# Chunked attention with a softplus feed-forward layer: the seven output products in another order, w_out's sums on GpSimd, output quarters on its queue

## The chip, the core and the metric

The kernel runs on one core of one Trainium2 chip. The metric is the device time of one execution in microseconds (us); lower is better. The engines are PE (TensorE, matrix products), DVE (VectorE), ACT (ScalarE), POOL (GpSimd) and SP, which here only issues transfers. A name with a small q behind it (SPq, ACTq, POOLq) is an engine's instruction queue, from which transfers are issued in order.

## The reference

Attention is taken within chunks of 64 positions; its output, as 4608 rows of 512, goes through a feed-forward layer of width 2048 with softplus.

```python
scores = scale * np.matmul(q_c, k_c.transpose(0, 1, 2, 4, 3))
scores = scores - np.max(scores, axis=-1, keepdims=True)
attn = np.exp(scores)
attn = attn / (np.sum(attn, axis=-1, keepdims=True) + 1e-09)
out = np.matmul(attn, v_c)
...
h = x @ w_in
g = np.maximum(h, 0.0) + np.log1p(np.exp(-np.abs(h)))
return (g @ w_out).astype(np.float32)
```

## The kernel before

Every float32 product is made of three: an operand is split into a rounded part (hi, cast by ScalarE) and a remainder (lo, a subtraction on VectorE or GpSimd), and hi·hi + lo·hi + hi·lo are summed in PSUM. The 4608 rows are nine blocks of 512. Three blocks are done plainly (`gemm1`, `gemm2`); the other six in three stages of two blocks each, n = 0, 1, 2. In a stage the first product, x @ w_in, is done by a scheme with seven products of half-size operands instead of eight: `product(w, k)`, task P0 to P6, for eight pairs j = 0 to 7 of w_in's column blocks. Its operands are seven sums of x (`x_sum`, `x_hi`, `x_lo`; tasks xs, xH, xL, kept in `wi_hi`/`wi_lo` for k below 4 and in three of the four `wib` tiles above) and seven sums of w_in that lie in a DRAM scratch and are loaded for each pair from GpSimd's queue (`ring_load`, line 745). `mix` (line 807; two of its six sums on GpSimd, the others on VectorE) puts each pair's products together, `soft` (line 816) applies softplus; in stages 0 and 1 the second block's result is spilled to DRAM, loaded back (`spill_load`, line 825, task ul, on SP's queue), and goes through `gemm2` (task G2, its remainder by line 660) after the eight pairs.

The last stage, n = 2 (`BOTH`), does the second product, g @ w_out, by seven products too: `sum_product(k, j)`, line 947, task R{k}_{j}, k = 0 to 6, eight j each. Its g operands are made in place from the four softplus blocks of pair j, u_block(j, i, c) (`t_sum`, line 904, tasks ts1 to ts4; `g_hi`, line 927; `g_lo`, line 931). Its w_out operands are: the plain halves, and four sums per j (`v_total`, line 871, task vt, two per j; `v_sum`, line 881, vs0 to vs3; `v_hi`, line 885, on ScalarE; `v_lo`, line 890, vl0 to vl3). VectorE makes all vt; vs and vl go to GpSimd for even j, to VectorE for odd j. Sum 0 stays in SBUF (`first_image`) for R1; the other sums (`v_store`, line 893, task vd) and copies of the plain halves (`own_image`, line 866) go to a DRAM tensor, `images`, and are loaded back per product (`image_load`, line 897, task wr) on SP's queue. The tiles `eT`, `qe`, `ka` and `ends` hold the sums, and later softplus blocks of pairs 5 to 7.

PE's order is written out as `seq`. In stage 2 it is, per pair j: P0 to P6, one of the two G2 left over from stage 1 (behind pair 0 and pair 1), and for j above 1 R0 and R1 of j - 2. Behind pair 7: R0, R1 of 5, 6 and 7, then R2 to R5, then R6 in two column halves, whose last piece is cut in two (RZ0, RZ1). Two PSUM accumulators of two tiles are shared (`ACC`); `set_by` (task keep), `combine` (sum) and `out_turn` (turn, line 975, a transpose on VectorE) take the four output quarters from them: b after R3, d after R4, a after R5, c21 after R6. `out_store` (line 986, task put) stores a quarter's half `ct` in four transfers of 64 KB, in runs of 32 floats. All of b, d, a and the first half of c21 go from SP's queue; the last half, in two parts of 32 KB transfers, alternately from SP and ACT.

All other engines' orders come from class `Plan`: it runs through the tasks with given costs and urgencies (`urg`, lower first) and emits each engine's instructions in the order that this gives. The order of emission is fixed in the kernel; an engine waits at the instruction that stands next.

## Time and profile before

| what | us |
|---|---|
| median of 3 runs | 841.07 |
| lowest, highest | 840.05, 845.37 |
| the profiled execution | 840.33 |
| its span, from the first to the last instruction | 838.5 |
| PE busy in it | 808.7 (96%) |
| VectorE, ScalarE, GpSimd busy | 594.8, 404.5, 343.9 |

Times in the profile count from the span's start. Busy PE includes matmul ends that are modelled. A chain of waits is followed back from the last instruction, at each step to what released it; in this profile 81% of it is PE. "Idle before" in a group is the time that the engine stood idle just ahead of it, with what ended it.

### The profile page before, as it was taken

What the parts mean: (1) busy time and instruction counts of PE and PEld (TensorE: products, weight loads), DVE (VectorE), ACT (ScalarE), POOL (GpSimd) and SP (SyncE); (2) the same over time, 40 slices, a digit from 0 to 9 for tenths busy, and PEclk for the clock granted to TensorE, in tenths of its full rate; (3) what the DMA queues carried; (4) which work ended last, traced back from release to release, by engine and by line L of the source; (5) the groups of instructions that cost most, each with busy time, mean ns of one, the idle gap of its engine ahead of it and who ended that gap; (6) DMA issues with size and microseconds to landing.
All of it is one profiled execution on the core that took longest, in us unless ns stands there. A gap on an engine that the chain in (4) does not pass through costs nothing.

```text
span 838.5 us, 15563 instructions
## 1 busy us (share of the span) xinstructions
PE 808.7 (96%) x5675; PEld 660.2 (79%) x5675; DVE 594.8 (71%) x985; ACT 404.5 (48%) x667; POOL 343.9 (41%) x395
## 2 busy tenths in 40 slices
PE   8799999999999999999999999999999999899994
PEld 6687878887878888887888878888888777687883
DVE  4898985267477778565578886574777999748771
ACT  3767855443434574353443543444345454545450
POOL 1567569778975712212324111311303376321000
PEclk9999999999999999999999999999999999999998
DMA  9986758642674455776569647678374387753573
GB/s 214 249 222 172 219 147 272 183 113 72 176 171 114 106 155 203 203 214 169 164 199 226 169 139 223 169 208 215 118 229 138 112 303 286 250 174 115 165 187 51
DMA packets 215677, 151.27 MB, mean 180 GB/s; under 512 B 173296, under 2 KB 190960, under 8 KB 211376
## 3 DMA queue, kind: packets, MB, share of 16 engines
q1 hardware_dynamic: 204048, 101.37, 45.2%
q0 software_dynamic: 10464, 48.77, 17.8%
q8 instruction: 45, 0.74, 0.4%
q14 instruction: 32, 0.26, 0.1%
q10 hardware_dynamic: 1088, 0.13, 0.1%
HBM read 106.95 MB, written 41.94 MB: 178 GB/s over the span
## 4 chain that ended last, share of the span: by engine, by line
PE 81%; DVE 8%; ACT 3%; DMA 2%; SPq 2%; issue 2%; POOL 0%; DVEq 0%; POOLq 0%; ACTq 0%
PE po L1006 32%; PE pa L788 22%; PE pa L644 14%; PE po L947 9%; PE pa L608 2%; SPq L359 2%; PE pa L520 1%; DVE wib L807 1%; DVE g_lo L660 1%; DMA xb<-scratch 1%; DMA raw<-in_moe_w_out_dram 1%; DVE ends L881 1%; DMA spill<-ends 1%; DVE raw L871 0%; DVE g_lo L931 0%
## 5 line engine op out<-in xcount | busy, mean ns | idle before, releaser
L807 POOL TENSOR_TENSOR wib<-wib 128x512 f32<-128x512 f32 x48 | 64.8, 1349 | 232.8 <-ACT wib L794 211.3
L1006 PE MATMUL po<-late,g_hi 128*128 128x512 f32 x420 | 128.8, 392 | 0.0
L544 DVE STREAM_TRANSPOSE eT<-qe 32x256 f32<-32x256 f32 x216 | 93.9, 435 | 3.0
L788 PE MATMUL pa<-wi_hi,xb 128*128 128x512 f32 x304 | 94.1, 391 | 1.8 <-DVE wib L807 0.7
L1006 PEld LDWEIGHTS po<-late,g_hi 128*128 128x128 f32 x420 | 78.3, 188 | 16.4
L788 PE MATMUL pa<-wib,xb 128*128 128x512 f32 x360 | 87.2, 395 | 1.9 <-ACT wib L794 1.2
L1006 PE MATMUL po<-late,g_lo 128*128 128x512 f32 x224 | 83.7, 391 | 2.6 <-DVE g_lo L660 2.6
L1006 PE MATMUL po<-wo_hi,g_hi 128*128 128x512 f32 x224 | 85.0, 396 | 0.0
L1006 PE MATMUL po<-wo_lo,g_hi 128*128 128x512 f32 x224 | 83.7, 390 | 0.0
L1006 PE MATMUL po<-wo_hi,g_lo 128*128 128x512 f32 x224 | 83.7, 390 | 0.0
L788 PEld LDWEIGHTS pa<-wib,xb 128*128 128x128 f32 x360 | 66.0, 188 | 20.2 <-ACT wib L794 6.2
L652 ACT ACTIVATE u<-pa 128x512 f32<-128x512 f32 (+1 forms) x50 | 29.0, 581 | 99.9 <-PE pa L644 93.0
L807 DVE TENSOR_TENSOR wib<-wib,pa 128x512 f32<-128x512 f32 x72 | 49.4, 686 | 33.9 <-PE pa L788 19.6
L656 ACT CAST g_hi<-ends 128x512 fp32r<-128x512 f32 x64 | 39.5, 616 | 65.4 <-PE po L1006 57.4
L660 DVE TENSOR_TENSOR g_lo<-ends,g_hi 128x512 fp32r<-128x512 f32 x64 | 45.7, 714 | 33.4 <-ACT g_hi L656 33.2
L788 PEld LDWEIGHTS pa<-wi_hi,xb 128*128 128x128 f32 x304 | 56.8, 188 | 14.9 <-DVE wib L807 1.2
L794 ACT COPY wib<-pa 128x512 f32<-128x512 f32 x72 | 39.8, 587 | 50.9 <-PE pa L788 50.9
L788 PE MATMUL pa<-wi_lo,xb 128*128 128x512 f32 x152 | 59.2, 389 | 0.0
L660 DVE TENSOR_TENSOR g_lo<-u,g_hi 128x512 fp32r<-128x512 f32 (+1 forms) x32 | 32.5, 1015 | 29.3 <-ACT g_hi L656 23.7
L1006 PEld LDWEIGHTS po<-late,g_lo 128*128 128x128 f32 x224 | 42.1, 188 | 12.4 <-DVE g_lo L660 3.7
L1006 PEld LDWEIGHTS po<-wo_hi,g_lo 128*128 128x128 f32 x224 | 42.1, 188 | 8.8
L1006 PEld LDWEIGHTS po<-wo_lo,g_hi 128*128 128x128 f32 x224 | 42.2, 188 | 8.6
(332 smaller groups left out, 1736.1 us busy)
## 6 DMA issues: line engine op xcount, KB each, us to landing
xb<-scratch POOLq DMA_DIRECT2D x19, 1024.0 KB, 5.9
xb<-scratch POOLq DMA_DIRECT2D x20, 768.0 KB, 7.1
raw<-in_moe_w_in_dram SPq DMA_DIRECT2D x16, 512.0 KB, 5.2
raw<-in_moe_w_out_dram SPq DMA_DIRECT2D x16, 512.0 KB, 4.5
scratch<-ends SPq DMA_DIRECT2D x16, 512.0 KB, 3.1
out_dram<-raw SPq DMA_DIRECT2D x28, 256.0 KB, 4.1
spill<-ends SPq DMA_DIRECT2D x14, 512.0 KB, 4.8
ends<-spill SPq DMA_DIRECT2D x14, 512.0 KB, 4.5
```

The costliest lines, as they stand in the source:

```text
L359: eng.dma_start(dst[p0 : p0 + rows], src[b, :, s0 : s0 + rows, :].rearrange("h s d -> s h d"))
L544: nc.vector.transpose(live["eT", i][d : d + BL, tb], e[s : s + BL, kb])
L608: nc.tensor.matmul(pa[o, a, col : col + C], vt[r, 4 * j + 2 * h2 + c2, :], eT[r, :, 4 * c2 + 2 * j + h2, :], start=True, stop=True,)
L644: nc.tensor.matmul(ph, wt[:, c, :], x[:, ts_, c, :], start=(n == 0), stop=(n == 3 * KC - 1))
L652: nc.scalar.activation(w["u"], w["ph"], AF.Softplus)
L656: nc.scalar.copy(w["hi"], w["u"])
L660: (nc.gpsimd if pool else nc.vector).tensor_tensor(w["lo"], w["u"], w["hi"].bitcast(F32), op=ALU.subtract)
L788: nc.tensor.matmul(w["bank"][BANK[k]], wts[:, q, c, :], x[:, c, :], start=k < NX and c + n == 0, stop=c == 1 and n == 2, skip_group_check= ...
L794: nc.scalar.copy(tmp_of(n), w["bank"][n])
L807: (nc.gpsimd if what in MIX_POOL else nc.vector).tensor_tensor(out, a, b, op=op)
L947: nc.tensor.matmul(live["acc", ACC[k]][ct][:, cols], (w[:, q] if k > 1 else w[q])[:, ct * P : (ct + 1) * P], g[:, cols], start=k in (0, 1, ...
L1006: nc.tensor.matmul(pos[w["m"]][t], terms[n][0][:, j * P : (j + 1) * P], terms[n][1], start=(w["first"] and n == 0), stop=n == 2 and (w["la ...
```

## The change

- `sum_product` takes as k = 0 and k = 1 the two plain halves of w_out, `wo[2j]` and `wo[2j + 1]`, with u_block(j, 0, 0) and u_block(j, 1, 0) as they come out of softplus. The products with sums are k = 2 to 5, and k = 6 has the plain half once more from `images`. ts1 to ts4 now serve k = 2, 3, 5 and 6. The accumulators are shared in another order (`ACC`, `set_by`, `combine`).
- R1 and R0 of pair j - 1 stand behind pair j (before: of j - 2), both left-over G2 behind pair 0, and R1, R0 of 6 and 7 behind pair 7. R5 of the last three j is split by output half (`SPREAD`).
- All vt, vs and vl go to GpSimd. For j = 0 to 3 they are made once P5 and P6 of stage 1's last pair are done, in `wib1` and `wib2`, the tiles that then take the sums of x of k = 5 and 6 for stage 2; these wait for the stores vd of j = 0 to 3. For j = 4 to 7 they are made in the three `raw` tiles, once the output rows of the last block of stage 1 are stored. All four sums of a j are stored now, and vs of a j waits for the stores of the j before it in its stage. `own_image` stores only half of what it did.
- The softplus blocks lie elsewhere: pair 0 in `ends`, pair 1 in `eT` and `qe`, pair j above 1 in w_out's tiles of j - 2.
- Quarters a, c, d (c in place of b) are stored from GpSimd's queue, c21 alternately from SP's and ACT's.

The diff, cut to its core:

```diff
+    SUM_OF = (2, 3, 5, 4)
+    def own_image(j, q):
+        on("wo").dma_start(images[6, :, j, q, :], wo[2 * j + 1][q].bitcast(F32)[:, HC:])
...
+    def v_space(j):
+        at = SUM_AT[j]
+        if ("v space", at) not in live:
+            if at in SUM_RAW:
+                live["v space", at] = [raw_tile(n, True) for n in range(3)]
+                a, b = (later.tile([P, 4 * MT], F32, name=f"wib{n}") for n in (1, 2))
+                live["v space", at] = [a[:, : 2 * MT], a[:, 2 * MT :], b[:, : 2 * MT], b[:, 2 * MT :]]
+        return live["v space", at]
...
-        live["vt", j, b] = raw_tile(0)[:, b * DM : (b + 1) * DM] if j % 2 else blk_tile("eT")
-        nc.vector.tensor_tensor(live["vt", j, b], hi, lo, op=ALU.add)
+        space = v_space(j)
+        t = space[j % (len(space) - 2)]
+        live["vt", j, b] = t[:, b * DM : (b + 1) * DM]
+        (nc.vector if j in VT_DVE else nc.gpsimd).tensor_tensor(live["vt", j, b], hi, lo, op=ALU.add)
...
-        t = ends.bitcast(F32)[:, n * MT : (n + 1) * MT] if j % 2 else blk_tile(("qe", "ka")[n % 2])
+        t = v_space(j)[n // 2 - 2][:, n % 2 * MT : (n % 2 + 1) * MT]
-        (nc.vector if j % 2 else nc.gpsimd).tensor_tensor(live["vs", j, n][:, 1], a, b, op=op)
+        (nc.vector if j in V_DVE else nc.gpsimd).tensor_tensor(live["vs", j, n][:, 1], a, b, op=op)
...
-    OF_G = ((0, 0), (0, 0), (0, 0), (1, 1), (0, 1), (1, 0), (0, 0))
+    OF_G = ((0, 0), (1, 0), (0, 0), (0, 0), (1, 1), (0, 1), (1, 0))
-    ACC = (0, 1, 0, 1, 0, 1, 0)
+    ACC = (0, 1, 1, 0, 1, 0, 0)
...
-            w = (wo[2 * j], [first_image(j)[:, q] for q in range(2)])[k]
+            w = wo[2 * j + k]
...
-                start=k in (0, 1, 5) and j == 0 and n < len(cts), stop=j == FC // 2 - 1 and n >= 2 * len(cts),
+                start=k < 3 and j == 0 and n < len(cts), stop=j == FC // 2 - 1 and n >= 2 * len(cts),
...
-        nc.scalar.copy(saved(what, ct), live["acc", 1 if what == "d" else 0][ct])
+        (nc.vector.tensor_copy if what == "a" and ct else nc.scalar.copy)(
+            saved(what, ct), live["acc", int(what != "c")][ct]
+        )
...
-        nc.vector.tensor_tensor(to, to, saved("c", ct) if what == "d" else live["acc", 1][ct], op=ALU.add)
+        nc.vector.tensor_tensor(to, to, live["acc", int(what == "c")][ct], op=ALU.add)
...
+    def put_queue(what, ct, cb):
+        return PUT[what, ct][cb % len(PUT[what, ct])]
...
-        eng = nc.sync if part is None else (nc.sync, nc.scalar, nc.sync, nc.scalar)[cb]
+        eng = {"ACT": nc.scalar, "SP": nc.sync, "POOL": nc.gpsimd}[put_queue(what, ct, cb)]
...
+    SUM_AT = (1, 1, 1, 1, 2, 2, 2, 2)
+    SUM_RAW = (2,)
+    VT_DVE = ()
+    V_DVE = ()
+    R_LAG = 1
+    SPREAD = 3
+    VD_URG = 60
+    OWN_URG = -100
+    PUT = {(w, ct): ("POOL",) for w in "acd" for ct in range(2)}
+    PUT.update({("c21", ct): ("SP", "ACT") for ct in range(2)})
...
-            seq += [f"G2_{v_['name']}" for v_ in behind[1:]] if n not in BOTH else []
-            if n in BOTH and w["j"] > 1:
-                seq += [f"R{k}_{w['j'] - 2}" for k in range(2)]
-            behind = behind[1:] if n in BOTH else w["first"][::-1]
+            seq += [f"G2_{v_['name']}" for v_ in behind[1:]]
+            if n in BOTH and R_LAG <= w["j"] < FC // 2 - 1:
+                seq += [f"R{k}_{w['j'] - R_LAG}" for k in (1, 0)]
+            behind = [] if n in BOTH else w["first"][::-1]
...
-            seq += [f"R{k}_{FC // 2 - 2 + j}" for j in range(2) for k in range(2)]
-            seq += [f"R{k}_{j}" for k in range(2, 6) for j in range(FC // 2)]
+            NJ = FC // 2
+            seq += [f"R{k}_{j}" for j in range(NJ - R_LAG - 1, NJ) for k in (1, 0)]
+            seq += [f"R{k}_{j}" for k in range(2, 6) for j in range(NJ if k < 5 else NJ - SPREAD)]
+            seq += [f"R5_{j}{ct}" for ct in range(2) for j in range(NJ - SPREAD, NJ)]
...
+            if k > 4:
+                gone = gone + [f"vd{j}_{i}" for j in range(FC // 2) if SUM_AT[j] == n - 1 and n - 1 not in SUM_RAW for i in range(4)]
...
+                if j > 1:
+                    needs += [f"R{i}_{j - 2}", f"vt{j - 2}_{i}"] + [f"own{j - 2}{q}" for q in range(2)] * i
+                elif j:
+                    needs += [f"B{tag(list(bursts)[-1])}_{b}" for b in range(2)]
                 else:
-                    needs += [f"v{'d' if f else 'l'}{FC // 2 - 1 - b}_{f}" for b in range(2) for f in range(4)]
+                    needs += [f"lo{v_['name']}" for w_ in pairs[at - FC // 2 : at] for v_ in w_["second"]]
...
+            d = due((at, 1, 0)) + 8 * nth if at not in SUM_RAW else A + 25 + 10 * nth
+            eng, cost = ("DVE", 0.42) if j in V_DVE else ("POOL", 0.75)
+            if at in SUM_RAW:
+                free = [f"st{SUPERS[n] - 1}_{t}" for t in range(TPM)] + [f"B{tag(list(bursts)[-1])}_{i}" for i in range(2)]
+                free += [f"x{q}{n}_0" for q in "HL"]
+                wide = 1
+            else:
+                free = [f"P{k}_{pairs[FC // 2 * (at + 1) - 1]['name']}" for k in (5, 6)]
+                wide = 2
             for b in range(2):
-                plan.add(f"vt{j}_{b}", "DVE", 0.69, partial(v_total, j, b), [f"w_{h}{of_out[2 * j + b]}" for h in ("hi", "lo")] + before_, urg=d)
+                needs = [f"w_{h}{of_out[2 * j + b]}" for h in ("hi", "lo")] + free
+                if nth >= wide:
+                    needs += [f"vs{mine[nth - wide]}_{i}" for i in range(4)]
+                pool = j not in VT_DVE
+                plan.add(f"vt{j}_{b}", "POOL" if pool else "DVE", 1.4 if pool else 0.69, partial(v_total, j, b), needs, urg=d)
...
+                needs += [f"vd{mine[nth - 1]}_{i}"] if nth else []
...
-                if i:
-                    plan.add(f"vd{j}_{i}", QUEUE["wo"], ISSUE[QUEUE["wo"]], partial(v_store, j, i), [f"vl{j}_{i}"], urg=d + 5, kb=215)
+                plan.add(f"vd{j}_{i}", QUEUE["wo"], ISSUE[QUEUE["wo"]], partial(v_store, j, i), [f"vl{j}_{i}"], urg=d + VD_URG, kb=215)
...
-                t = {1: 1, 2: 2, 4: 3, 6: 4}.get(k)
+                t = {2: 1, 3: 2, 5: 3, 6: 4}.get(k)
...
-                        past = {2: ["keepa0", "keepa1"], 3: ["keepd0", "keepd1"], 4: ["keepb0", "keepb1"], 5: ["sumb0", "sumb1"],
-                                6: ["keepc0", "keepc1"]}
+                        past = {2: ["keepa0", "keepa1"], 3: ["suma0", "suma1"], 4: ["keepd0", "keepd1"], 5: ["keepc0", "keepc1"], 6: [f"sumd{ct}"]}
...
+            for what, end, urg in (("a", f"R0_{e}", B + 2), ("c", f"R4_{e}", B + 36), ("d", f"R5_{e}{ct}", -3)):
+                plan.add(f"sum{what}{ct}", "DVE", 0.69, partial(combine, what, ct), [end, f"keep{what}{ct}"], urg=urg)
+                plan.add(f"turn{what}{ct}", "DVE", 0.66, partial(out_turn, what, ct),
+                         [f"sum{what}{ct}"] + [f"vd{j}_{i}" for j in range(NJ) if SUM_AT[j] in SUM_RAW for i in range(4)], urg=urg + 4 if urg > 0 else B + 50)
                 for cb in range(4):
-                    plan.add(f"put{what}{ct}{cb}", "SP", 0.57, partial(out_store, what, ct, cb), [f"turn{what}{ct}"], urg=1e5, kb=100)
...
-            plan.add(f"putc210{cb}", "SP", 0.57, partial(out_store, "c21", 0, cb), ["turnc210"], urg=1e5, kb=100)
-                eng = ("SP", "ACT", "SP", "ACT")[cb]
+                    eng = put_queue(what, ct, cb)
+                    plan.add(f"put{what}{ct}{cb}", eng, ISSUE[eng], partial(out_store, what, ct, cb), [f"turn{what}{ct}"], urg=1e5, kb=100)
```

## Rows read from the trace of the kernel before

**Rows 1.** Stretches: length, busy PE, PEld, DVE, ACT, POOL (count), clock, DMA, GB/s

```profile
641.00:661.93 20.93, 19.99 (x109) 16.07 (x100) 20.91 (x19) 11.82 (x19) 11.58 (x8) 1.00 0.50 161
661.93:763.65 101.72, 97.75 (x422) 77.95 (x421) 79.38 (x113) 50.18 (x100) 50.37 (x54) 1.00 0.63 222
763.65:827.04 63.39, 63.38 (x279) 51.60 (x278) 45.23 (x71) 30.55 (x54) 0.00 (x0) 1.00 0.48 137
```

**Rows 2.** Timeline after 815, three engines: start, us, engine, line, operation, out<-in

```profile
817.13 1.30 DVE L975 STREAM_TRANSPOSE raw<-wib 128x512 f32<-128x512 f32 x2
...
817.87 13.79 SPq L986 DMA_DIRECT2D out_dram<-raw  x8
...
827.55 1.89 ACTq L986 DMA_DIRECT2D out_dram<-k  x4
...
833.94 1.94 SPq L986 DMA_DIRECT2D out_dram<-k  x4
```

**Rows 3.** Waits of SP's queue after 600: total us, times, longest us

```profile
SPq L825 <- DVE g_lo L660: 26.8, 6, 7.0
...
SPq L986 <- DMA out_dram<-k: 9.9, 1, 9.9
```

**Rows 4.** Waits of PE, 640 to 728, columns as before

```profile
PE pa L788 <- ACT wib L794: 1.9, 2, 1.2
...
PE pa L788 <- DVE wib L807: 1.1, 2, 0.7
...
PE pa L788 <- ACT ends L885: 1.0, 1, 1.0
```

**Rows 5.** Busy time of lines 871, 881, 890 alone, 661.93 to 722.50

```profile
661.93:722.50 60.57, 14.84 (x14) 1.00 0.71 259
...
661.93:722.50 60.57, 9.22 (x16) 10.13 (x12) 1.00 0.71 259
...
661.93:722.50 60.57, 7.14 (x16) 10.13 (x12) 1.00 0.71 259
```

**Rows 6.** Chain of waits, 750 to 764: start us, us, what

```profile
751.24 2.76 PE po L947 x12
...
754.00 9.65 PE pa L788 x42
```

**Rows 7.** Timeline of VectorE, 750 to 756

```profile
754.66 0.69 DVE L931 TENSOR_TENSOR g_lo<-eT,g_hi 128x512 fp32r<-128x512 f32 x1 [1.21 <-ACT g_hi L927]
```

**Rows 8.** GpSimd's groups, 120 to 340: busy us, mean ns; idle before

```profile
L716 POOL TENSOR_TENSOR ends<-raw 128x256 f32<-128x256 f32 x32 | 24.8, 805 | 0.6
...
L704 POOL TENSOR_TENSOR raw<-wi_hi,wi_lo 128x512 f32<-128x512 f32 x8 | 10.2, 1286 | 0.9 <-DMA scratch<-raw 0.8
```

**Rows 9.** Busy time, 120 to 300, columns as in Rows 1

```profile
120.00:300.00 180.00, 176.18 (x1556) 145.14 (x1546) 115.91 (x201) 81.77 (x127) 142.55 (x173) 1.00 0.58 154
```

**Rows 10.** Line 660, whole run: duration ns min/median/max

```profile
L660 DVE TENSOR_TENSOR g_lo<-ends,g_hi x64: 653/692/1227, 328.3 to 662.4; 128x512 fp32r<-128x512 f32 x64
...
L660 DVE TENSOR_TENSOR g_lo<-u,g_hi x32: 414/693/4783, 32.1 to 315.0; 128x512 fp32r<-128x512 f32 x29, 128x256 fp32r<-128x256 f32 x3
```

**Rows 11.** Line 881 on GpSimd, whole run: duration ns min/median/max

```profile
L881 POOL TENSOR_TENSOR qe<-eT x8: 742/876/1646, 642.7 to 712.1; 128x256 f32<-128x256 f32 x8
...
L881 POOL TENSOR_TENSOR ka<-eT,ka x4: 720/939/1710, 648.8 to 713.5; 128x256 f32<-128x256 f32 x4
```

**Rows 12.** Start of the third stage: timeline of VectorE

```profile
665.95 1.22 DVE L775 TENSOR_TENSOR wib<-xa,wib 128x1024 fp32r<-128x1024 f32 x1
```

**Rows 13.** Line 893's stores, whole run: time from issue to landing

```profile
DMA to landing us min/median/max: 2.0/4.3/7.1
```

**Rows 14.** GpSimd's DMA issues of lines 371 and 479: ns min/median/max

```profile
L371 POOL DMA_DIRECT2D raw<-in_v_dram x28: 617/618/656, 146.4 to 442.9; - x28
...
L479 POOL DMA_DIRECT2D k<-in_k_dram x1: 1127/1127/1127, 102.6 to 102.6; - x1
```

**Rows 15.** Line 745's loads, GpSimd's queue: time from issue to landing

```profile
DMA to landing us min/median/max: 4.6/6.3/10.0
```

More of the change, by code (lines that the diff above doesn't have):

```diff
@@ L219, in chunked_attention_softplus_ffn @@
     wi = [tuple(const.tile([P, HALF_FC, KC, P], F32R, name=n) for n in ("wi_hi", "wi_lo"))]
-    stage = [later.tile([P, 4 * MT], F32, name="wib") for _ in range(4)]
+    stage = [later.tile([P, 4 * MT], F32, name=f"wib{n}") for n in range(4)]
     wo = [tuple(const.tile([P, DM], F32R, name=f"wo_{n}{fc}") for n in ("hi", "lo")) for fc in range(HALF_FC)]
@@ L313, in wi_of @@
         if n == len(wi):
-            wi.append(tuple(later.tile([P, 4, KC, P], F32R, name="wib") for _ in range(2)))
+            wi.append(tuple(later.tile([P, 4, KC, P], F32R, name=f"wib{2 * n - 2 + i}") for i in range(2)))
         return [w[:, fc - (0, HALF_FC, HALF_FC + 4)[n]] for w in wi[n]]
@@ L670, in high @@
     def high(n):
-        if "high" not in live:
-            live["high"] = [later.tile([P, 4 * MT], F32R if j < 3 else F32, name="wib") for j in (0, 1, 2, 3)]
-        return live["high"][n]
+        if ("high", n) not in live:
+            live["high", n] = later.tile([P, 4 * MT], F32R if n < 3 else F32, name=f"wib{n}")
+        return live["high", n]
     def x_image(k):
@@ L1470, in add_sums @@
         NJ = FC // 2
-        gone = [f"B{tag(list(bursts)[-1])}_{i}" for i in range(2)]
         for j in range(NJ):
             for q in range(2):
-                for b in range(1, 2):
-                    plan.add(f"own{j}{q}{b}", QUEUE["wo"], ISSUE[QUEUE["wo"]], partial(own_image, j, q, b),
-                             [f"w_{'lo' if q else 'hi'}{of_out[2 * j + b]}", f"G2_{pairs[FC // 2 * (j // 4)]['second'][0]['name'] + 4 * (j % 4) + 2 * q}"], urg=A - 200 + 3 * j, kb=225)
+                plan.add(f"own{j}{q}", QUEUE["wo"], ISSUE[QUEUE["wo"]], partial(own_image, j, q),
+                         [f"w_{'lo' if q else 'hi'}{of_out[2 * j + 1]}", f"G2_{pairs[FC // 2 * (j // 4)]['second'][0]['name'] + 4 * (j % 4) + 2 * q}"], urg=A + OWN_URG + 3 * j, kb=115)
@@ L1507, in add_sums @@
                 else:
-                    needs = [f"own{j}{q}{int(k > 0)}" for q in range(2) for j in half]
-                end = f"R{k}_{half[-1]}" if k < 6 else ("R6_31", "RZ1")[part]
+                    needs = [f"own{j}{q}" for q in range(2) for j in half]
+                end = f"R{k}_{half[-1]}" + ("1" if (k, part) == (5, 1) else "") if k < 6 else ("R6_31", "RZ1")[part]
                 plan.add(f"wr{k}_{part}", QUEUE["image"], ISSUE[QUEUE["image"]], partial(image_load, k, part), needs + ([f"wr{k}_0"] if part else []),
@@ L1564, in add_sums @@
[L1564 to L1571 removed]
+            for what, k in (("a", 1), ("d", 2), ("c", 3)):
+                on_dve = what == "a" and ct
+                plan.add(f"keep{what}{ct}", "DVE" if on_dve else "ACT", 0.69 if on_dve else 0.6, partial(set_by, what, ct),
+                         [f"R{k}_{e}"] + ([f"P4_{last}", f"c11_{last}", f"soft00_{last}", f"soft11_{last}"] if k == 1 else []), urg=-4)
@@ new lines, in add_sums @@
+        for ct in range(2):
+            for z in range(2) if ct else (None,):
+                name = "c21" + str(ct) + ("" if z is None else "ab"[z])
+                plan.add("turn" + name, "DVE", 0.75 if z is None else 0.45, partial(out_turn, "c21", ct, z), [f"R6_{e}0" if z is None else f"RZ{z}"], urg=-3)
+                for cb in range(4):
+                    eng = put_queue("c21", ct, cb)
+                    plan.add(f"put{name}{cb}", eng, ISSUE[eng], partial(out_store, "c21", ct, cb, z), ["turn" + name], urg=1e5, kb=50 if ct else 100)
```

115 lines of the change are left out of this document (35 added, 80 removed).

## Prediction

> **What bounds the kernel now.** Read the page first: PE is busy almost throughout, so time can come only from the gaps of PE and from what lies behind its last product. The table by stretch shows where these are [rows 1]. From 763.65 PE runs 63.38 of 63.39 us: R2 to R6 have no gap and give nothing. From 661.93 to 763.65, the eight pairs of the last stage, PE is busy 97.75 of 101.72. From 641 to 661.93, the last G2 of stage 1, it loses 0.94. And after PE's last product, at 827.04, 11.46 us pass to the end of the span, 838.5.
>
> Next, the timeline of the end [rows 2]. SP's queue holds eight stores of quarter a from 817.87 for 13.79 us; then come the first half of c21 and, last, four stores of its second half, until 833.94 + 1.94 = 835.88. ACT's queue, which had nothing ahead, issued its own four by 827.55 + 1.89 = 829.44. The waits of SP's queue say why [rows 3]: one store on SP waited 9.9 us for a store of c21 on ACT to land, a transfer of a later quarter. So SP stood until c21's end was there, and only then sent what had been ready at 818.43 (the end of a's transposes, 817.13 + 1.30).
>
> Last, the gaps inside the pairs: PE waits 1.9 for ScalarE and 1.1 for VectorE at line 788, and 1.0 that the profile puts down to line 885 [rows 4], in all 4.0. In just that stretch VectorE spends 14.84 us on vt, 9.22 on vs and 7.14 on vl, 31.2 of 60.57 [rows 5].
>
> **The end.** The change leaves SP and ACT twelve stores, those of c21, in the order in which they become ready; a, c, d go by GpSimd's queue. What ACT shows, four small stores in 1.89 us with nothing ahead, then holds for both queues: two of each part on each. The last issue would end at 829.44 on this execution's clock; from the last issue to the end before it was 838.5 - 835.88 = 2.62; 829.44 + 2.62 = 832.06, against 838.5: **6.4 us less**. SP's image loads are unaffected: they come before.
>
> The stores on GpSimd's queue must be done by then. Nothing else stands there from 763.65 on [rows 1]. Their issue has no row for 64 KB in runs of 128 bytes, which is 512 runs. A 64 KB load of 256 runs took 0.62 us on that queue, one of 1024 runs 1.13 [rows 14]; between the two I take 0.77, nearer the small one. The last quarter, d, has its transposes done as late as a has now: R5 still stands in front of R6, so 8.6 us before PE's end (827.04 - 818.43). Eight stores take 6.2, and landing 6.3, the median of that queue's big loads [rows 15]: 3.9 after PE's end, against the 5.0 of c21 (832.06 - 827.04). It fits by 1.1 us. At 1.13 each and the slowest landing, 10.0, they end 10.4 after PE and the end gains only 1.0. The other bound is 6.9, if c21's stores issue half a microsecond faster than ACT's did.
>
> Against moving them speaks a rule: the Trainium skill, SBUF — State Buffer, section "SBUF: two separate sides", says that a transfer issued from GpSimd has its descriptors written by GpSimd, which VectorE can lock out while it runs certain copies. The trace does not show it: 28 issues took 617 to 656 ns [rows 14]. By the rule the end would gain 1.0 or less.
>
> **The pairs.** Undisturbed, seven products take 9.65 us and twelve matmuls behind them 2.76 [rows 6]. Eight of the first and seven of the second (two G2, five couples of R) make 96.5; the stretch takes 101.7, so 5.2 are lost. The work of PE itself is the same after the change; one couple of R only moves from behind the last pair into the pairs. The change takes the 31.2 us off VectorE. What comes to GpSimd instead: for four j, eight vt at 1.29 and 32 vs and vl at 0.81 [rows 8], 36.1 us, against 20.3 now (10.13 twice) [rows 5]. GpSimd also makes two of the six sums of `mix`, which can now stand behind a vt of 1.29. The first of them may start about one product after P2 and is used after P5, two products (2.8 us) later; with 1.29 of its own and 1.29 ahead it is still in time, so I count nothing. VectorE loses half its queue in that stretch; ScalarE's stays, but it is busy half of the time only (50.18 of 101.72), so it was late because of what it waited for. I take **4.0 back of 5.2**, bounds 0 (the waits turn to GpSimd) and 5.2. The second G2 behind pair 0 also gives pair 1's loads 2.7 us more.
>
> **The seam behind pair 7.** R0 of pair 7 now stands three products behind the pair instead of four to six. With nothing in the way the chain from a pair's last product to its g_lo is 754.66 + 0.69 - 751.24 = 4.1 us [rows 6, 7]; three products are 4.1 (half of 2.76 each). It is tight; I put **0.5 us** on it, bounds 0 and 1.4 (one product's length).
>
> **Sums beside G2.** The sums of j = 0 to 3, 36.1 us of GpSimd, now run from about 610 beside stage 1's last G2, whose remainders (line 660) VectorE reads from two SBUF tiles. Such a remainder takes 0.69 us, up to 1.23 in this form, and in the first blocks once 4.78, with GpSimd at work [rows 10]. The nearest stretch is 120 to 300: GpSimd busy 142.55 us, with just such sums of w_in, and PE short of full by 3.8 [rows 9]. That is 0.027 per us, **1.0 us** here; bounds 0 and 5 (one remainder of 4.78 in place of 0.69, and a few smaller).
>
> **Sum.** 840.33 (the profiled execution) - 6.4 - 4.0 + 0.5 + 1.0 = **831.4 us**. That execution is 0.7 under the median of the three runs, less than the runs differ; I leave the number as it is.
>
> **Rivals.**
>
> 1. *The first-stage sums come too late; slower.* x's sums 5 and 6 for the last stage take the place of j = 0 to 3's sums, so P5 of pair 0 waits until these are stored. P5 starts 661.93 + 5 × 1.38 = 668.8; after the last landing a ScalarE cast and a VectorE remainder of 1.22 [rows 12] follow, about 2.5 in all. The point is a landing at 666.3. From 610: 36.1 of work, three waits of one j's sums for the stores of the j before, and a landing of 4.3, at most 7.1 [rows 13]. Those stores stand in SP's queue among the seven loads of spill, where SP now stands up to 7.0 at a time behind line 660 [rows 3]. With 3 × 7.0 and 7.1 it lands at 674.2, 7.9 late: 839.3. With GpSimd's sums at the long row, 1.7 for 256 columns [rows 11], it is 68 us of work and 19.1 late: 850.5, slower by 1.1%. For it: SP's queue is a chain of waits there. Against: a store usually lands in 4.3 while the next j's totals and remainders, 5 us, still run. Any landing before 666.3 costs nothing.
> 2. *The waits in the pairs only change their name*: GpSimd, at 36 us and `mix`, becomes what PE waits for. 840.33 - 6.4 + 1.5 = 835.4. For it: 15 us more on GpSimd in the same stretch. Against: `mix` on GpSimd is not the last wait in any gap now [rows 4].
> 3. *All gaps go*: 840.33 - 6.4 - 5.2 - 0.9 = 827.8. For it: VectorE is so much freer. Against: the 0.94 before 661.93 comes while x's sums run beside GpSimd, and GpSimd is no less busy after.
> 4. *GpSimd's stores end last*, the end gains 1.0: 840.33 - 1.0 - 4.0 + 1.5 = 836.8.
> 5. *Nothing comes of it*: SP's stores still wait for another queue's, and the gaps stay: 840.3.
>
> **How the numbers follow.** Forecast 0.50 (its own range 829 to 834.5: each term half way to its bounds), rival 1 0.10, rival 2 0.17, rival 3 0.13, rival 4 0.06, rival 5 0.04. The range 826 to 838 takes in the forecast and rivals 2, 3, 4 and leaves 0.14 out. About 1% is what a measurement of this kernel can tell from no change; the bounds are 832.66 and 849.5. Faster: four fifths of the forecast, rival 3 and a little of rival 2, 0.55. Slower: the far part of rival 1, 0.04. The rest, 0.41, is the same.
>
> **What would show it.** The end: from PE's last product to the span's end about 5 us, SP's last store beginning within 2.5 us of it, no wait of SP for a transfer of ACT's; GpSimd's last store landed before. The pairs: PE short by 1 to 2 us instead of 4, lines 871, 881, 890 absent from VectorE. The sums beside G2: remainders of line 660 longer than 0.69 between 610 and 650, PE short there by 1 us. Wrong would be: a gap at P5 of pair 0 or at pair 1's loads with line 893's stores ahead (rival 1); PE waiting for line 807 on GpSimd (rival 2); GpSimd issuing at 1.1 us or more near the end (rival 4); or SP's stores still waiting for another queue's transfer (rival 5).

## The result

The kernel after takes 830.8 us (median of 4 runs, 828.24 to 832.59), the kernel before, beside it on the same chip, 842.06. The ratio is 0.986, 95% interval 0.9817 to 0.9903. The prediction was 831.4, from 826 to 838. The profiled execution of the kernel after took 831.35 us, with a span of 829.6; it is the one that is read below. In what follows, lines have the numbers of the kernel after: 865, 875, 883 for 871, 881, 890 of before; 886 for 893; 879 for 885; 924 for 931; 940 for 947; 970 for 975; 984 for 986; 1004 for 1006.

### The profile page after: what moved, and what is told of

It is laid out like the page before. It is cut to its first block, busy times and chain, and to the rows that moved or that the text cites. A ratio compares the mean times of both kernels' runs of the same rounds, so it can differ in the third digit from the quotient of the medians.

```text
span 829.6 us, 15582 instructions
## 1 busy us (share of the span) xinstructions
PE 809.9 (98%) x5675; PEld 661.9 (80%) x5675; DVE 581.2 (70%) x938; ACT 403.2 (49%) x664; POOL 404.3 (49%) x467
## 4 chain that ended last, share of the span: by engine, by line
PE 77%; DVE 8%; DMA 4%; ACT 4%; POOL 3%; issue 3%; SPq 1%; DVEq 0%; POOLq 0%; ACTq 0%
PE po L1004 28%; PE pa L788 22%; PE pa L644 13%; PE po L940 9%; DVE g_lo L660 2%; PE pa L608 2%; DMA xb<-scratch 2%; PE pa L520 1%; DVE wib L807 1%; DMA images<-wib 1%; DVE ends L306 1%; POOL raw L875 1%; DVE eT L544 1%; DMA raw<-in_moe_w_in_dram 1%; POOL raw L865 1%
## 5 line engine op out<-in xcount | busy, mean ns | idle before, releaser
L807 POOL TENSOR_TENSOR wib<-wib 128x512 f32<-128x512 f32 x48 | 63.0, 1312 | 207.9 <-ACT wib L794 198.5
L788 PE MATMUL pa<-wi_hi,xb 128*128 128x512 f32 x304 | 93.9, 390 | 0.4 <-DMA xb<-scratch 0.4
L788 PE MATMUL pa<-wib,xb 128*128 128x512 f32 x360 | 87.2, 395 | 0.7 <-DVE wib L775 0.7
L788 PEld LDWEIGHTS pa<-wib,xb 128*128 128x128 f32 x360 | 65.9, 188 | 18.7 <-ACT wib L794 4.5
L660 DVE TENSOR_TENSOR g_lo<-ends,g_hi 128x512 fp32r<-128x512 f32 x64 | 53.3, 832 | 29.3 <-ACT g_hi L656 29.0
L788 PEld LDWEIGHTS pa<-wi_hi,xb 128*128 128x128 f32 x304 | 56.8, 188 | 13.1 <-issue 1.4
L788 PE MATMUL pa<-wi_lo,xb 128*128 128x512 f32 x152 | 59.2, 389 | 0.0
```

Source lines behind the costliest of these rows:

```text
L660: (nc.gpsimd if pool else nc.vector).tensor_tensor(w["lo"], w["u"], w["hi"].bitcast(F32), op=ALU.subtract)
L788: nc.tensor.matmul(w["bank"][BANK[k]], wts[:, q, c, :], x[:, c, :], start=k < NX and c + n == 0, stop=c == 1 and n == 2, skip_group_check= ...
L807: (nc.gpsimd if what in MIX_POOL else nc.vector).tensor_tensor(out, a, b, op=op)
```

## The profile after

First the same three stretches as in [rows 1], with the same columns, cut where the stages end here: the last G2 of stage 1, the eight pairs, the products R behind them.

```profile
641.00:664.52 23.52, 23.21 (x159) 18.77 (x160) 21.52 (x18) 13.46 (x23) 14.59 (x13) 1.00 0.56 186
664.52:764.00 99.48, 98.96 (x433) 80.34 (x433) 55.60 (x63) 46.26 (x88) 65.71 (x70) 1.00 0.61 214
764.00:824.62 60.62, 60.57 (x268) 49.31 (x266) 48.52 (x78) 28.90 (x50) 15.47 (x24) 1.00 0.53 153
```

The pairs now take 99.48 us and hold one couple of R (R1 and R0 of one j) more. PE is short of full by 0.52 there, where it was short by 3.97. VectorE is busy 55.60 us in place of 79.38, GpSimd 65.71 in place of 50.37. PE ends at 824.62, the span 4.98 later; before, 11.46 lay between.

The end, in order of time, answers to [rows 2]: start us, us, engine, line, operation, out<-in.

```profile
817.84 5.13 POOL L984 DMA_DIRECT2D out_dram<-raw  x8 [6.67 <-DVE wi_lo L924]
...
819.92 0.89 SPq L984 DMA_DIRECT2D out_dram<-q  x2
...
824.64 0.78 DVE L970 STREAM_TRANSPOSE k<-po 128x256 f32<-128x256 f32 x2 [4.75 <-PE po L940]
825.12 1.81 SPq L984 DMA_DIRECT2D out_dram<-k  x4
825.12 1.90 ACTq L984 DMA_DIRECT2D out_dram<-k  x4
```

Both queues begin c21's last four stores at once, 0.50 behind PE's last product. GpSimd issued its last eight in 5.13 us, 0.64 each, and was done at 822.97. The waits of PE from 605 on (total, times, longest) are these two, where [rows 4] had three in the pairs alone:

```profile
PE po L1004 <- DVE g_lo L660: 1.0, 2, 0.7
PE pa L788 <- ACT wib L794: 0.5, 1, 0.5
```

The waits of SP's queue, which answer to [rows 3]. No store of line 984 waits for another queue's transfer any more; what SP's stores of sums wait for is GpSimd:

```profile
SPq L886 <- POOL raw L883: 58.2, 16, 13.8
...
SPq L825 <- DVE g_lo L660: 11.1, 7, 3.8
SPq L886 <- POOL wib L883: 11.1, 9, 4.7
```

Last, the groups of line 660 from 608 to 641, beside stage 1's last G2: first of the kernel before, then of the kernel after (busy us, mean ns of one; idle before).

```profile
L660 DVE TENSOR_TENSOR g_lo<-ends,g_hi 128x512 fp32r<-128x512 f32 x11 | 7.6, 689 | 6.9 <-ACT g_hi L656 6.8
```

```profile
L660 DVE TENSOR_TENSOR g_lo<-ends,g_hi 128x512 fp32r<-128x512 f32 x10 | 13.9, 1392 | 1.4 <-ACT g_hi L656 1.3
```

The remainder that VectorE takes there has become twice as long. In 608 to 641 GpSimd's busy time went from 0.53 to 28.08 us, and VectorE's from 22.65 to 29.77, though it has no instruction more.

## The experiments

To compare stages, I count from one mark: the last start of the row `L788 PE MATMUL pa<-wib,xb` before 640, the end of stage 1's last P. It stands at 607.7 us in the kernel before and at 608.9 in the kernel after, and between 606.2 and 610.6 in the kernels below (two aside, which were slower from the start). This spread of some 4 us comes from the first 320 us, in which nothing was changed. Counted from the mark, the stages vary less, but not by nothing: up to pair 0 the three kernels with the order of before agree (54.1 us each), while the kernel after and the one with SP's stores, which have the same instructions in the same order there, take 55.5 and 54.7.

**The stores alone.** The kernel before, with only the queues changed (here, and in the planner's entries for these stores):

```diff
-        eng = nc.sync if part is None else (nc.sync, nc.scalar, nc.sync, nc.scalar)[cb]
+        eng = nc.gpsimd if what != "c21" else (nc.sync, nc.scalar)[cb % 2]
```

> The kernel before with one part of the change: quarters b, d, a are stored from GpSimd's queue and c21 alternately from SP's and ACT's; the order of the products and the engines of the sums stay. If the end is worth what was predicted, PE ends where it did (about 827) and the span ends about 5.0 us behind it in place of 11.5: about 834 to 836 us, ratio 0.992. If the end gained because R5's last products were split and the quarters come in another order, the end stays over 8 us long and the time over 837.

It took 833.8 us, ratio 0.9924 (0.9905 to 0.9942): 6.4 us less. PE ends at 765.60 + 63.39 = 828.99, the span at 834.0, 5.0 later. The last stores begin in both queues together, as in the kernel after:

```profile
821.37 5.13 POOL L986 DMA_DIRECT2D out_dram<-raw  x8 [4.49 <-DVE wi_lo L931]
...
829.49 1.82 SPq L986 DMA_DIRECT2D out_dram<-k  x4
829.49 1.90 ACTq L986 DMA_DIRECT2D out_dram<-k  x4
```

The end's term stands by itself, with no other part of the change needed.

**No store on ACT.** The kernel before with c21's last half on SP as well, nothing on GpSimd. It asks whether SP stood because of ACT's transfer.

```diff
-        eng = nc.sync if part is None else (nc.sync, nc.scalar, nc.sync, nc.scalar)[cb]
+        eng = nc.sync
```

> The kernel before with c21's last half stored from SP alone, nothing on ACT and nothing on GpSimd. If SP stood for 9.9 us because a store of its own waited for a transfer of ACT's, that wait is gone: SP issues a's eight stores from 818 on, the first half of c21 at 822, and then eight small stores from 827.5 on at 0.47 each; the last issue ends 3.8 behind the turn, the span about 6.9 behind PE's end, 835 to 837 us. If SP was held by its own rate or by transfers in flight, it still ends 11 us or more behind PE: 840 or more.

It took 835.97 us, ratio 0.9948 (0.9933 to 0.9963). SP's queue waits for no transfer of another queue's any more, and the span ends 6.9 behind PE (825.60, span 832.5):

```profile
808.09 13.50 SPq L986 DMA_DIRECT2D out_dram<-raw  x16
821.69 2.11 SPq L986 DMA_DIRECT2D out_dram<-q  x4
826.10 3.77 SPq L986 DMA_DIRECT2D out_dram<-k  x8
```

So the 9.9 us were the wait for ACT's transfer and not SP's own work. Taking the help of a second queue away made the kernel before 4 us faster.

**The kernel after with SP's stores.** Quarters a, c, d and the first half of c21 from SP, the last half from SP and ACT, as in the kernel before:

```diff
-    PUT = {(w, ct): ("POOL",) for w in "acd" for ct in range(2)}
-    PUT.update({("c21", ct): ("SP", "ACT") for ct in range(2)})
+    PUT = {(w, ct): ("SP",) for w in "acd" for ct in range(2)}
+    PUT.update({("c21", 0): ("SP",), ("c21", 1): ("SP", "ACT")})
```

> The changed kernel with its stores on the queues of before: quarters a, c, d and the first half of c21 from SP, the last half alternately from SP and ACT. If the queues are what shortened the end, PE ends where it does in the changed kernel (about 824.6) and 9 to 11.5 us follow in place of 5.0: about 835 to 838 us, with a store of SP waiting for one of ACT. If the new order of the quarters would have done it alone, the end is 5 to 6.5 us long and the time at most 833.

It took 833.78 us, ratio 0.9926 (0.991 to 0.9942). PE ends at 768.87 + 54.49 = 823.36, the span at 831.8: 8.4 later, less than expected, for the wait is back at half its length.

```profile
SPq L984 <- DMA out_dram<-k: 5.0, 1, 5.0
```

```profile
823.87 1.89 ACTq L984 DMA_DIRECT2D out_dram<-k  x4
825.52 1.95 SPq L984 DMA_DIRECT2D out_dram<-q  x4
```

SP issued c21's first half behind the stores of its second half on ACT. Why a transfer of SP's waits for one of ACT's that the kernel doesn't make it wait for, no row says. It was there in both kernels in which SP and ACT shared one half while SP had earlier stores ahead, and in none of the others; that is as far as it is shown.

**The engines as before.** The kernel after with the sums shared out as in the kernel before: all vt on VectorE, vs and vl of odd j too.

```diff
-    VT_DVE = ()
-    V_DVE = ()
+    VT_DVE = tuple(range(8))
+    V_DVE = (1, 3, 5, 7)
```

> The changed kernel with the sums of w_out on the engines of before (all vt on VectorE, vs and vl of odd j on VectorE, of even j on GpSimd), at the places of the changed kernel. If VectorE's relief is what closed PE's gaps in the pairs, the pairs lose 2 to 5 us again, while the last G2 of the stage before, beside less GpSimd work, lose 1 to 2.6 us less: 831 to 835 us. If PE's order (both G2 behind pair 0, a couple of R one pair earlier) closed them, the pairs stay within 1 us of full and the time falls to 828 to 830.

It took 834.3 us, ratio 0.9934 (0.9912 to 0.9956). The pairs take 104.81 us, from 664.17 to 768.98, and PE has its waits again:

```profile
PE pa L788 <- DVE wib L775: 1.8, 1, 1.8
PE pa L788 <- DVE wib L807: 1.0, 1, 1.0
PE pa L788 <- ACT wib L794: 0.7, 1, 0.7
```

Of the 5.3 us more in the pairs, 1.7 are the clock: behind the first of these waits the granted clock is 0.50 (1.2 GHz) from 673.9 to 677.3, where it is 1.00 in the kernel after. The order of the products, the second couple behind each pair and the two stages of the sums are all in this kernel, and it is no faster than the one with the stores alone (834.3 against 833.8). In this order of products the gaps close when VectorE's 31 us go; the order of before with the sums on GpSimd was not run.

**All sums in the last stage.**

```diff
-    SUM_AT = (1, 1, 1, 1, 2, 2, 2, 2)
+    SUM_AT = (2, 2, 2, 2, 2, 2, 2, 2)
```

> The kernel after with all eight j of w_out's sums in the last stage (SUM_AT all 2), so that GpSimd makes nothing of them beside stage 1's last G2. Theory (the two stages are what lets GpSimd take the sums over: G2 pays 1.4 us for it, and in the last stage GpSimd has room for four j only): the 1.4 us beside G2 go, pair 0 starts 54.3 us after the last matmul of stage 1's last P (in the kernel after 55.6, in the kernel before 54.2). In the last stage GpSimd, busy 63 of 98 us in the kernel after with 36 us of sums, would need 63 + 36 = 99 us: the sums of the last j end 10 us or more late and the images of R2 with them, which PE needs from about 767 on. Median 836 to 845. Rival A (GpSimd has room all the same, its waits hide): PE has no new wait, median 829.4. Rival B (GpSimd does mix between the sums and mix comes late): the gaps stand inside the pairs, at line 788 for GpSimd, 4 us or more, and R2 has none; 834 to 838.

It took 859.02 us, ratio 1.0223 (1.0198 to 1.0247): the theory, and worse than its numbers.

```profile
PE po L940 <- DMA xb<-images: 23.2, 1, 23.2
```

GpSimd's last remainders begin at 791.57 and take 3.43, where PE stood ready at 777.7. I had R2's second half due at 772 to 773; it is due at 777, since two couples of R stand behind pair 7. Even with that slack the sums ended 17 us too late, their store and the load not counted. The granted clock is down too, behind a PE that had stood idle: 0.50 (1.2 GHz) from 800.9, where PE starts again, to 805.9, so some 2.5 us more are lost there. Made in the last stage alone, GpSimd's sums come too late for R2.

**Six and two, five and three.** The same line, with two and with three j in stage 1.

```diff
+    SUM_AT = (1, 1, 2, 2, 2, 2, 2, 2)
```

> The kernel after with two j of the sums in stage 1 and six in the last stage. Theory (in the last stage there is room for one j more than the kernel after has, not for two; with all eight there R2 waited 23.2 us): GpSimd's last sum ends at about 774, PE waits for the image of R2's second half, from 772 to 783, some 10 us; the loss beside G2 falls to 54.2. Median 839. Rival (the planner's order is what held the sums back, and GpSimd has room): no wait for an image, median 829.5.

It took 834.17 us, ratio 0.9931 (0.9908 to 0.9954). GpSimd's last sum ends at 773.2, as expected; but of the wait for the image only 1.9 us were left, as R2's second half is due at 777.

```diff
+    SUM_AT = (1, 1, 1, 2, 2, 2, 2, 2)
```

> The kernel after with three j of w_out's sums in stage 1 and five in the last stage, all on GpSimd. GpSimd loses a quarter of its sums beside G2 (9 of 36 us) and has 9 more in the pairs. Theory: the loss beside G2 shrinks with GpSimd's time there (55.5 us from the last matmul of stage 1's last P to pair 0 become 54.7); in the last stage a j takes GpSimd some 14 us among its other work, so the last sum ends at about 760 in place of 745.8; its store and the load of the image take 10, so the image is there at 770, just before R2's second half wants it at 772. Median 830.0. Rival A (GpSimd's mix is held up in the pairs): pairs over 100.5, median 832. Rival B (R2's image comes late): a wait of PE for the image of 3 us or more, median 834.

It took 831.69 us, ratio 0.9901 (0.9874 to 0.9928), which are rival A's numbers (pairs over 100.5, median 832), though it is not GpSimd's part of `mix` that is held up but VectorE's. No image is late. Beside G2 it is 2.0 us better than the kernel after (53.5 against 55.5 from the mark to pair 0), in the pairs 4.3 worse. The largest piece of that is one place, in order of time on three engines:

```profile
739.43 7.61 DVE L924 TENSOR_TENSOR g_lo<-wo_hi,g_hi 128x512 fp32r<-128x512 f32 x2 [1.52 <-ACT g_hi L920]
740.03 2.11 POOL L883 TENSOR_TENSOR raw<-raw 128x256 f32<-128x256 f32 x3
...
744.61 1.28 POOL L807 TENSOR_TENSOR wib<-wib 128x512 f32<-128x512 f32 x1
...
749.15 2.32 PE L788 MATMUL pa<-wib,xb 128*128 128x512 f32 x6 [2.44 <-DVE wib L807]
```

Two remainders of VectorE, 0.69 each when nothing is beside them, take 7.61 us; they end 1.15 behind GpSimd's run of instructions, which ends at 745.89. `mix` stands behind them on VectorE, and PE waits 2.44 for it. Behind that wait the granted clock is 0.50 from 749.9 to 753.3, which costs 1.7 more.

**The totals on VectorE, in stage 1.** Eight vt of 1.29 off GpSimd, beside G2 only.

```diff
-    VT_DVE = ()
+    VT_DVE = (0, 1, 2, 3)
```

> The kernel after with the totals vt of the first four j on VectorE (VT_DVE = 0 to 3); the sums vs and the remainders vl stay on GpSimd. Theory (what PE loses beside stage 1's last G2 is VectorE's remainder held up behind GpSimd instructions that follow one another without a break: totals of 1.29 us, three in a row): GpSimd loses 8 x 1.29 = 10.3 us there, VectorE gets 8 x 0.69 = 5.5. From the last matmul of stage 1's last P to the start of pair 0 it takes 54.3 us (kernel after 55.6, before 54.2, and 54.3 in the kernel with all engines as before), longest remainder of line 660 there under 2 us; nothing changes behind it. Median 829.5. Rival A (it is the sums vs and vl on GpSimd, or the traffic, not the totals): still 55.6, median 830.8. Rival B (VectorE is the engine that is short there, and has 5.5 us more to do): 57 or more, median 832 to 834.

It took 832.53 us, ratio 0.9898 (0.9879 to 0.9916). No remainder of line 660 in 608 to 641 is longer than 1.22 us, yet from the mark to pair 0 it is 56.5, longer than before the edit: rival B, near enough. The theory has fallen in this form: the long remainders went and the time did not come back.

**Stage 1 as before, the last stage on GpSimd.**

```diff
+    VT_DVE = (0, 1, 2, 3)
+    V_DVE = (1, 3)
```

> The kernel after with stage 1's sums alone shared out between the engines as before: the totals vt of the first four j on VectorE, and vs and vl of j = 1 and 3 too; the last stage's sums all on GpSimd, as in the kernel after. Theory A (beside G2 it is GpSimd's time that makes VectorE's two-SBUF remainders long; with GpSimd at some 20 us there instead of 43 the loss goes, as it did in the kernel with all engines as before): from the last matmul of stage 1's last P to pair 0 54.1 us (kernel after 55.5), the pairs stay at 99.5, median 829.4. Theory B (VectorE is short there whichever way the work is shared, as the totals alone on VectorE showed with 56.5): 56 to 57, median 832.

It took 830.84 us, ratio 0.9892 (0.9869 to 0.9915); from the kernel after it can't be told. Theory A holds for G2: 54.1 from the mark to pair 0. But the 1.4 us come back at pair 0, which takes two waits of PE, 1.8 and 0.5 us, for x's remainders of line 775: VectorE came to the first of them late, behind the sums of j = 3, and beside GpSimd's `mix` (2.72 us from 667.09) took 2.29 us for it in place of 1.22.

```profile
668.59 2.29 DVE L775 TENSOR_TENSOR wib<-xa,wib 128x1024 fp32r<-128x1024 f32 x1
...
670.94 1.73 PE L788 MATMUL pa<-wib,xb 128*128 128x512 f32 x6 [1.77 <-DVE wib L775]
```

**Breaks in GpSimd's run.** Behind each vt, vs and vl a memset of one column, which reads nothing (80 in the trace, of some 95 ns).

```diff
+    gap = const.tile([P, 1], F32, name="gap")
+    def break_run():
+        nc.gpsimd.memset(gap, 0.0)
...
+        break_run()
```

> The kernel after with one tiny instruction more behind each of GpSimd's totals, sums and remainders of w_out (a memset of one column, which reads nothing): 72 instructions more on GpSimd, no work taken away. Theory (a remainder of VectorE that reads two SBUF tiles does not get in between GpSimd instructions that read SBUF and follow one another without a break, and gets in at the first break): the remainder of 3.48 us at 612 and its like go, none in 608 to 641 is longer than two of GpSimd's instructions (2.0 us), their mean there falls from 1392 ns to some 1000; from the last matmul of stage 1's last P to pair 0 54.5 us (kernel after 55.5); median 830 or a little less, though GpSimd has more to do. Rival (the long remainders are GpSimd's share of the memory, breaks or not): mean 1392 ns or more, 55.5 us or more, median 831 to 833 for the time of the added instructions.

It took 844.28 us, ratio 1.0035 (1.0022 to 1.0049), and the same with the split of three and five:

> The split of three j in stage 1 and five in the last stage, with the same tiny instructions behind GpSimd's totals, sums and remainders. Without them one pair of VectorE's remainders took 7.61 us (739.43), from within a run of GpSimd's instructions to its end, and PE waited 2.4 us for a sum behind them. Theory (the run without a break is the cause): that wait goes, the pairs take 100 to 101.5 us in place of 104.0, median 829 to 830. Rival (VectorE is late for the fifth j's sake, or the added instructions break nothing): pairs 104 or more, median 831.7 or more.

It took 847.96, ratio 1.0077 (1.0057 to 1.0098), and kept the wait (2.6 for 2.4). Neither says anything on the question by its time, since both were slower from the first products on: the mark stands at 620.6 and 621.5. Their rows do, and they are the rivals': the first kernel has a remainder of 3.40 as well, at 624.46, the same mean of line 660 as the kernel after when the window is moved with the mark (1392 ns, 619.7 to 652.7), and 55.2 us from the mark to pair 0. The second has the pair of long remainders again, 8.17 for 7.61:

```profile
755.65 8.17 DVE L932 TENSOR_TENSOR g_lo<-wo_hi,g_hi 128x512 fp32r<-128x512 f32 x2 [1.51 <-ACT g_hi L928]
```

So memsets of 95 ns break nothing. What made both slower, and whether longer breaks do more, the last run asks.

**Longer breaks, and a tile of another size.**

```diff
+    gap = const.tile([P, BL * 2], F32, name="gap")
+    def break_run():
+        for _ in range(4):
+            nc.gpsimd.memset(gap, 0.0)
...
         (nc.vector if j in VT_DVE else nc.gpsimd).tensor_tensor(live["vt", j, b], hi, lo, op=ALU.add)
+        break_run()
```

> The kernel after with four short instructions that read nothing (memsets of 64 columns) behind each of GpSimd's 16 totals only, into a tile of 256 bytes per partition, where the kernel with breaks had one of 4 bytes. Two questions. First, why all was slower with the tile of 4 bytes, from the first products on (512-column matmuls of 395 to 396 ns in place of 389): if it is that the tile moved every later tile by 4 bytes, the matmuls are back at 389 ns and the last matmul of stage 1's last P is at 607 to 611 again; if it is the tile or the memsets as such, 395 ns and 620. Second, whether a longer break lets VectorE in where one memset of 93 ns did not (3.40 us): with breaks of some 0.4 us between the three totals at 609 VectorE's first remainder of line 660 there takes at most 2.0 us and the way to pair 0 54.5 us, median 830; if GpSimd's memsets hold VectorE out as its sums do, 3.4 us or more, 55.5 us or more, median 831 to 833.

It took 837.61 us, ratio 0.9955 (0.993 to 0.998). The mark is back at 606.2, and VectorE does get in. From GpSimd and VectorE (lines stand six or seven further on than in the kernel after):

```profile
609.51 0.78 POOL L864 MEMSET gap<- 128x64 f32 x4
610.25 1.69 POOL L871 TENSOR_TENSOR wib<-wo_hi,wo_lo 128x512 f32<-128x512 f32 x1
```

```profile
610.10 0.69 DVE L660 TENSOR_TENSOR g_lo<-ends,g_hi 128x512 fp32r<-128x512 f32 x1 [1.26 <-ACT g_hi L656]
```

The remainder that took 3.48 us takes 0.69, and it is GpSimd's next total that is held up, 1.69 for 1.29. The mean of line 660 in 608 to 641 falls from 1392 to 944 ns. And still the way to pair 0 is 59.8 us, 4.3 more than in the kernel after. ScalarE and PE show the first of two places:

```profile
616.03 0.41 ACT L886 CAST wib<-wib 128x256 fp32r<-128x256 f32 x1 [2.24 <-POOL wib L882]
616.35 0.62 ACT L656 CAST g_hi<-ends 128x512 fp32r<-128x512 f32 x1
```

```profile
619.26 0.50 PE L1011 MATMUL po<-late,g_lo 128*128 128x512 f32 x1 [1.51 <-DVE g_lo L660]
```

ScalarE stands 2.24 us at the cast of a sum that GpSimd has not made yet; the cast of G2's block stands behind it in the same queue, then VectorE's remainder, which itself takes 2.21 beside GpSimd, then PE. So these 1.5 us come from a GpSimd that the breaks made later and from a longer remainder, together. The second place is larger: PE waits 2.2 for a remainder at 651.14, in a chain of waits that goes back over x's sums on VectorE to a load of spill, and then runs at a granted clock of 0.50 from 651.3 to 654.7, 1.7 more.

## Why the prediction came out

**The end.** Predicted 5.0 us from PE's last product to the span's end, measured 4.98, by the mechanism named: SP's and ACT's queues hold c21 only, and go in step. With the stores alone the gain is 6.4, the term's own size. Two of its parts were too dear. A 64 KB store took GpSimd 0.64 us and not the 0.77 taken, and landed in 3.2 (median; 5.7 at most) and not 6.3. So GpSimd's last store lands some 1.6 us behind PE (822.97 + 3.2 - 824.62), 4.1 at most, always ahead of the span's end at 4.98. Rival 4 had no case. Nor was the rule that speaks against it seen, which the Trainium skill, SBUF — State Buffer, section "SBUF: two separate sides", states for stores issued from GpSimd beside certain copies of VectorE: 24 issues took 649 to 705 ns. That is no test of it, since VectorE ran none of those copies beside them, only operations on two tensors and transposes.

**The pairs.** Predicted 4.0 of 5.2 back. Undisturbed they would take 8 × 9.65 + 8 × 2.755 = 99.2; they took 99.48, so all but 0.2 came back. The cause named holds: with the engines as before the same pairs take 104.81, or 103.1 without the clock's 1.7. The size was off because I left 1.2 for waits that would change their name to GpSimd; none did (rival 2). Of the 31.2 us that left VectorE, though, its busy time shows only 23.8: beside GpSimd the remainders of line 924 that read two SBUF tiles got longer, 1589 ns on average for eight of them. They have time, since a couple of R stands a whole pair behind; PE waits for none of them. The Trainium skill, Perfetto Trace Analysis, section "Optimizing Scalar/DVE Operations", warns that to move work between GpSimd and VectorE might not help, since they share a read port. In the pairs it helped by 5 us all the same, beside G2 it did not.

**The seam.** Predicted +0.5, measured 0: from 764.00 to 824.62 there are 60.62 us; before there were 63.39, with one couple of 2.76 more.

**The sums beside G2.** Predicted +1.0, bounds 0 and 5; measured +1.4, as the way from the mark to pair 0 is 55.5 us against 54.1. The kernel with SP's stores, the same up to there, has 54.7, so the size is known to 0.8 only: +0.6 to +1.4. The reason named, longer remainders of VectorE, holds where PE waits longest, 0.7 us. From ScalarE, VectorE and PE:

```profile
631.36 0.62 ACT L656 CAST g_hi<-ends 128x512 fp32r<-128x512 f32 x1 [2.18 <-DMA ends<-spill]
632.40 1.20 DVE L595 TENSOR_TENSOR qe<-qe,den 128x512 f32<-128x512 f32 x1
633.53 1.23 DVE L660 TENSOR_TENSOR g_lo<-ends,g_hi 128x512 fp32r<-128x512 f32 x1
634.81 0.50 PE L1004 MATMUL po<-wo_hi,g_lo 128*128 128x512 f32 x1 [0.68 <-DVE g_lo L660]
```

Casts of line 656 and remainders of line 660 come one for one, so this remainder is that of the cast done at 631.98. VectorE, which between 612.74 and 642.07 never stands idle for 0.1 us, comes to it 1.55 later, and takes 1.23 for 0.69. What sets the two executions apart begins at one instruction of VectorE that also reads two SBUF tiles, 15.9 us behind the mark in both; first in the kernel after, then in the one with SP's stores:

```profile
624.76 1.22 DVE L595 TENSOR_TENSOR qe<-qe,den 128x512 f32<-128x512 f32 x1
```

```profile
624.25 0.68 DVE L595 TENSOR_TENSOR qe<-qe,den 128x512 f32<-128x512 f32 x1
```

In the second, GpSimd's sum beside it starts just after it, not before it, and is the one that takes longer (1.25 for 0.86). From there VectorE is 0.55 us earlier, 0.77 at the remainder shown, and PE has no wait at that place. But over all kernels neither the mean length of the remainders nor GpSimd's time orders the way to pair 0:

| kernel | mark to pair 0, us | mean of line 660, 608 to 641, ns | GpSimd busy there, us |
|---|---|---|---|
| all sums in the last stage | 52.8 | 689 | 1.2 |
| two and six | 53.0 | 1159 | 20.9 |
| three and five | 53.5 | 1247 | 27.7 |
| stage 1 as before | 54.1 | 792 | 8.9 |
| engines as before | 54.1 | 805 | 10.1 |
| before | 54.1 | 689 | 0.5 |
| after, SP's stores | 54.7 | 1373 | 29.4 |
| after | 55.5 | 1392 | 28.1 |
| totals on VectorE | 56.5 | 987 | 21.8 |
| longer breaks | 59.8 | 944 | 28.8 |

Steps of 0.8 us and less are not resolved in this table. With all sums in the last stage PE has no wait in the stretch, so 52.8 is its length undisturbed, and the kernel before loses 1.3 there already, around the 0.94 of the prediction. That a late sum of GpSimd reaches PE through ScalarE's queue is shown for the longer breaks alone, and there only in part. With the totals on VectorE the remainders got shorter and VectorE had more to do; why the kernels stand in just this order stays open.

Rival 1 had no case: SP's last store of the first four j issues at 659.1, and those from 655 on land in 4.2 at most, some 5 us before P5 of pair 0 could want it; no wait of PE stands there. Its far number takes all 40 of GpSimd's instructions at 1.7; with the eight vt at 1.29 the work is 65 us and not 68.

**The sum.** Against 838.5 the span is -6.5 at the end, -5.0 in the pairs, 0 at the seam, +1.4 beside G2 in this execution, and +1.2 up to the mark, where nothing was changed: -8.9, which is 829.6. The errors in the pairs (-1.0), in the seam (-0.5) and beside G2 (+0.4) and the late start (+1.2) nearly cancel, so that the 831.35 of the profiled run stands closer to 831.4 than the terms deserve.

**No version beats it.** Of the kernels tried, the one with stage 1 as before is as fast (830.84), the others are slower: what they won beside G2 came back at pair 0, in the pairs or at R2's image.

## What to carry to other kernels

Read, from the end back, which queue each of the last transfers stands in, and whether one queue waits for another's: here two queues that each held nothing but the last quarter were worth 6.4 us, and even one queue alone beat the shared one. When work moves to an engine off the path, look at two things: whether a neighbour that gets slower beside it has time left (beside G2 VectorE had none, and PE waited), and which in-order queues its results pass through (with the longer breaks a cast stood behind a late sum). Here the move from VectorE to GpSimd paid in the pairs, by 5 us, where the slower remainders are used a whole pair later, and cost 0.6 to 1.4 beside G2, where they are used at once. That this distance is what decides is my reading; no run varied it alone.

## What the runs showed of the hardware that was not expected

**VectorE can be held out through a run of GpSimd's.** The longest remainder of the kernel after, and GpSimd beside it:

```profile
612.74 3.48 DVE L660 TENSOR_TENSOR g_lo<-ends,g_hi 128x512 fp32r<-128x512 f32 x1 [1.26 <-ACT g_hi L656]
612.70 0.72 POOL L875 TENSOR_TENSOR wib<-wib 128x256 f32<-128x256 f32 x1
613.38 1.27 POOL L865 TENSOR_TENSOR wib<-wo_hi,wo_lo 128x512 f32<-128x512 f32 x1
614.62 0.73 POOL L875 TENSOR_TENSOR wib<-wib,wib 128x256 f32<-128x256 f32 x1
```

It ends at 616.22, behind these three and the first DMA issue in GpSimd's run (at 615.31). With three and five j two remainders take 7.61, to the end of the run; memsets of 95 ns between the sums change nothing (3.40 and 8.17), four of them, 0.78 us, let VectorE in at once (0.69). But this is the rarer case. Of the 19 remainders of lines 660 and 924 that took over 1 us in the kernel after between 608 and 764, 16 took under 1.8: they waited behind one instruction of GpSimd's at most, and most of them then held up its next one, though no break shows in its run there either:

```profile
639.64 0.74 POOL L875 TENSOR_TENSOR wib<-wib 128x256 f32<-128x256 f32 x1
639.69 2.38 DVE L660 TENSOR_TENSOR g_lo<-ends,g_hi 128x512 fp32r<-128x512 f32 x2
640.34 1.19 POOL L883 TENSOR_TENSOR wib<-wib 128x256 f32<-128x256 f32 x1
```

The Trainium skill, SBUF — State Buffer, section "Who interferes with whom", says that a VectorE instruction with two SBUF inputs contends with GpSimd instructions that read SBUF, that the lock on the shared ports is exclusive, and that the order of issue decides who blocks. The 16 agree, and so does line 595 above; the three of 3.16 to 3.48 waited behind several instructions, and what decides between the two cases is not shown.

**With a tile of 4 bytes per partition most products were slower.** With it, allocated ahead of other tiles, most matmuls of 512 columns took 395 to 396 ns, long before its first use at 621.5; with one of 256 bytes in its place they took 389. Line 788 in the kernels with a 4-byte and with a 256-byte tile (duration ns min/median/max):

```profile
L788 PE MATMUL pa<-wib,xb x288: 389/395/501, 329.0 to 620.6; 128*128 128x512 f32 x144
```

```profile
L788 PE MATMUL pa<-wib,xb x288: 388/389/499, 320.7 to 606.2; 128*128 128x512 f32 x144
```

That is 1.5% of a product; the mark came 12 us later than in the kernel after. Both kernels with the tile ran on one chip, but the kernel before, beside them, took 841.28 there, as elsewhere. That it comes from where the tiles lie, moved by 4 bytes, is the reading that is left, as the memsets come later; which operand's place counts was not tried.
